# A planner of instruction order that makes five passes, ranks steps by latest begin and counts transfers at 320 GB/s

## The chip, the core and the metric

The kernel runs on one core of a Trainium2 chip. The metric is the device time in microseconds of one execution of the whole program; lower is better.

## The reference

Causal attention with a cumulated bias over 4 batches, 8 heads, 576 positions and head size 64; its output, as 2304 tokens of 512 values, goes through two layers with weights 512 x 2048 and 2048 x 512. Cut to what is computed:

```python
def _attn_ref(q, k, v, s):
    scores = scale * np.matmul(q, k.transpose(0, 1, 3, 2))
    cum = np.cumsum(np.maximum(s, 0.0), axis=-1)
    bias = -(cum[:, :, :, None] - cum[:, :, None, :])
    scores = np.where(causal, -1000000000.0, scores + np.minimum(bias, 0.0))
    scores = scores - np.max(scores, axis=-1, keepdims=True)
    attn = np.exp(scores)
    attn = attn / (np.sum(attn, axis=-1, keepdims=True) + 1e-09)
    return np.matmul(attn, v)

def _moe_ref(x, w_in, w_out):
    h = x @ w_in
    return (np.maximum(h, 0.0) + np.log1p(np.exp(-np.abs(h)))) @ w_out

def _moe2_ref(x, w_in, w_out, a, b):
    h = x @ w_in
    h2 = h * h
    P = a[0] + a[1] * h + a[2] * h2 + a[3] * h2 * h
    Q = 1.0 + np.abs(b[0]) * np.abs(h) + np.abs(b[1]) * h2
    return (P / (Q + 1e-06)) @ w_out
```

The weights come in as 64-bit floats.

## The kernel before

**Stages.** Attention is cut into parts (Part), one for a head and a range of its rows, in five segments: rows 0 to 255 of batch 0 in plain float32 (tiles gh, gl hold their probabilities), the rest of batch 0, and then the other batches. A part is scores on TensorE (L511, or L513 and L514), a mask with a row minimum on VectorE (L491, L497, L500), an exponential with row sums on ScalarE (L504), the reciprocal of the sum on VectorE (L505, L506), the normalisation on GpSimd (L507), transposes on TensorE (L574, L578, L589, L594) with copies out of PSUM (L559, L564, L565) and the product with v (L637). The first layer takes tokens in tiles of 256, 256 and four of 448, the second in six of 384; each tile has 16 units, one for 128 of the 2048 hidden columns. A unit is stage_a (L892 to L894, x by w_in, 12 matmuls), the activation (stage1: L990 to L994; stage2, stage3: L1030, L1032) and stage_b (L928 to L930 or L935 to L937, by w_out). All operands of the layers are split in a high and a low part that together stand for a float32, so that each product is three matmuls.

**Weights.** A half of a unit's weights (128 x 512) is loaded by load_w (L743) and put together from its 64-bit form in conv1: L758 on GpSimd, L759 on ScalarE, L760 and L765 on VectorE, the high part L769 on ScalarE, the low part w1l L770 on GpSimd. Low parts are stored (L779) and loaded again for later tiles (stream_l, L789); both stand on SyncE's queue. The first eight units of tile 0 need 16 halves; then come eight units of tile 1, and then both in turn.

**What sets the order.** Each engine works through its own line in order. The program is traced part by part and unit by unit, and each instruction has a priority, which is its place in the trace, moved by offsets with tc.high_priority: C1_OFF = 50 for conversions of the first layer's weights, PRIO, P_S2, P_PREP, P_CUM, P_SPLIT, P_A, P_ST1, P_ST3 for others. At the end of the trace plan() (L169) simulates all engines. Step (L97) gives each instruction a price by its kind and size; depend() (L139) gives what must come before what. plan() takes, again and again, the step that can begin first on any engine; among those of one engine that can begin at the same time, the lowest priority number goes first. Buffers of a tag are given in the order of the trace. The lines that come out are tied as they are, by after(), for all steps that the model begins before 530 us (L1226); later ones are ordered by the framework's scheduler from their priorities. The instructions up to keep_order() (L358), among them the loads of the first heads and of the cumulated sums, are tied by hand. Prices that the prediction uses:

```python
SHARED = 0.7
DMA_RATE, DMA_LATENCY = 260e3, 1.9
...
            self.done = 0.1 + 0.00064 * n if one else 0.147 + 0.00106 * n
...
            self.done = 0.17 + 0.00215 * n if wide else 0.28 + 0.00075 * n
...
            slow = SHARED * s.port * port[other] * max(0.0, min(clock[other] - t, busy))
...
            dma = max(dma, clock[s.engine]) + s.dma / DMA_RATE
            done = dma + DMA_LATENCY
```

n is the number of elements of a partition; the first pair of prices is VectorE's, the second GpSimd's.

Of the kernel before, what the change touches and what calls it, by code (L numbers as in the profile page):

```python
# [54 lines left out]
PSUM_TAGS = ("acc", "h", "at")  # L55
LATENCY = {("Activation", "Pool"): 0.08, ("DVE", "Pool"): 0.19, ("PE", "DVE"): 0.09}
ISSUE = {"SP": 0.5, "Activation": 0.12}
SHARED = 0.7
DMA_RATE, DMA_LATENCY = 260e3, 1.9


class Access:
# [34 lines left out]
class Step:  # L97


    def __init__(self, i, tied):  # L100
        self.i, self.tied = i, tied
        self.engine = str(i.engine).split(".")[-1]
        acc = [[Access(x) for x in xs if getattr(getattr(x, "bass_ap", None), "tensor", None) is not None]
               for xs in (i.outs, i.ins)]
        self.outs, self.ins = acc
        self.dma = self.port = 0
        n = self.outs[0].elements if self.outs else 1
        psum = any(x.psum for x in self.outs + self.ins)
        wide = len(self.ins) > 1 and self.ins[1].dims[1][1] > 1
        if "DMA" in i.opcode:  # L110
            self.dma = 4 * n * self.outs[0].dims[0][1]
            self.busy = ISSUE.get(self.engine, 0.5)
        elif self.engine == "PE":
            turn = n == 128 and self.ins[0].tile.startswith("ident")
            full = not turn and "32r" not in str(i.ins[0].bass_ap.dtype)
            self.busy = 0.109 if turn else 0.024 + 0.00162 * n if full else 0.012 + 0.000428 * n
            self.done = self.busy + 0.165
        elif self.engine == "Activation":
            self.done = 0.175 + 0.00086 * n + 0.095 * max(0, len(self.outs) + len(self.ins) - 2)
            self.busy = self.done - 0.1  # L120
        elif self.engine == "DVE" and n == 1:
            self.busy, self.done = 0.115, 0.155
        elif self.engine == "DVE":
            one = len(self.ins) < 2 and not psum and i.opcode != "TensorCopy"
            self.done = 0.1 + 0.00064 * n if one else 0.147 + 0.00106 * n
            self.busy = self.done - 0.08
            self.port = 0 if psum else 1
        elif self.engine == "Pool":
            self.done = 0.17 + 0.00215 * n if wide else 0.28 + 0.00075 * n
            self.busy = self.done - 0.03  # L130
            self.port = 1 if wide else 0.4
        else:
            self.busy = self.done = 0.1
# [5 lines left out]
def depend(steps):  # L139

    names = {s.i.name: k for k, s in enumerate(steps)}
    preds = [{} for _ in steps]
    seen, first = {}, {}
    for k, s in enumerate(steps):
        def add(j, result):
            if j != k:
                preds[k][j] = result or preds[k].get(j, False)

        for x in s.ins + s.outs:
            if not x.ordered:  # L150
                continue
            write = x in s.outs
            for j, w, y in seen.get(x.tile, ()):
                if (write or w or x.psum and steps[j].engine != s.engine) and x.meets(y):
                    add(j, True)
        for x in s.ins + s.outs:
            write = x in s.outs
            if write:
                seen[x.tile] = [a for a in seen.get(x.tile, ()) if a[0] == k or not x.covers(a[2])]
            seen.setdefault(x.tile, []).append((k, write, x))  # L160
            if x.pool:
                add(first.setdefault(x.tile, k), False)
        for n in s.tied:
            if n in names:
                add(names[n], False)
    return preds


def plan(instructions, tied, until):  # L169

    steps = [Step(i, tied.get(i.name, ())) for i in instructions if i.opcode != "TilePoolBoundary"]
    preds = depend(steps)
    n = len(steps)
    succ = [[] for _ in steps]
    open_ = [len(p) for p in preds]
    for k, p in enumerate(preds):
        for j, result in p.items():
            succ[j].append((k, result))
    tiles = [s.tiles() for s in steps]
    pool, users, queue = {}, {}, {}  # L180
    for k, s in enumerate(steps):
        for x in s.ins + s.outs:
            if x.pool and x.tile not in pool:
                pool[x.tile] = x.pool
                queue.setdefault(x.pool[0], []).append(x.tile)
        for t in tiles[k]:
            users[t] = users.get(t, 0) + 1
    slots = {tag: [0.0] * bufs for tag, bufs in pool.values()}
    head = {tag: 0 for tag in slots}
    last = {tag: 0.0 for tag in slots}  # L190
    held, freed = set(), {}
    ready, start = [0.0] * n, [0.0] * n
    engines = sorted({s.engine for s in steps})
    clock = {e: 0.0 for e in engines}
    wait = {e: [k for k, s in enumerate(steps) if s.engine == e and not open_[k]] for e in engines}
    lines = {e: [] for e in engines}
    dma = 0.0
    port = {e: 0 for e in engines}

    def earliest(k):  # L200
        t, need = ready[k], {}
        for x in tiles[k]:
            if x not in held:
                tag = pool[x][0]
                need[tag] = need.get(tag, 0) + 1
                ahead = queue[tag][head[tag]:head[tag] + need[tag]]
                if any(y not in held and y not in tiles[k] for y in ahead):
                    return None
                free = sorted(slots[tag])
                if len(free) < need[tag]:  # L210
                    return None
                t = max(t, free[need[tag] - 1], last[tag])
        return t

    for _ in range(n):
        best = None
        for e in engines:
            can = [(max(t, clock[e]), steps[k].i.bass_priority, k) for k in wait[e]
                   for t in (earliest(k),) if t is not None]
            if can and (best is None or min(can)[0] < best[0]):  # L220
                best = min(can)
        t, _, k = best
        s = steps[k]
        wait[s.engine].remove(k)
        for x in tiles[k]:
            if x not in held:
                tag = pool[x][0]
                slots[tag].sort()
                slots[tag].pop(0)
                held.add(x)  # L230
                last[tag] = max(last[tag], t)
                while head[tag] < len(queue[tag]) and queue[tag][head[tag]] in held:
                    head[tag] += 1
        busy, done = s.busy, getattr(s, "done", 0.0)
        if s.port:
            other = "Pool" if s.engine == "DVE" else "DVE"
            slow = SHARED * s.port * port[other] * max(0.0, min(clock[other] - t, busy))
            busy, done = busy + slow, done + slow
        port[s.engine] = s.port
        start[k], clock[s.engine] = t, t + busy  # L240
        if s.dma:
            dma = max(dma, clock[s.engine]) + s.dma / DMA_RATE
            done = dma + DMA_LATENCY
        else:
            done += t
        lines[s.engine].append(k)
        for j, result in succ[k]:
            if not result:
                at = t
            elif steps[j].engine == s.engine == "PE":  # L250
                at = clock["PE"]
            else:
                at = done + LATENCY.get((s.engine, steps[j].engine), 0.04)
            ready[j] = max(ready[j], at)
            open_[j] -= 1
            if not open_[j]:
                wait[steps[j].engine].append(j)
        for x in tiles[k]:
            users[x] -= 1
            freed[x] = max(freed.get(x, 0.0), done)  # L260
            if not users[x]:
                slots[pool[x][0]].append(freed[x] + 0.04)
    return [[steps[k].i for k in line if start[k] < until] for line in lines.values()]


@with_exitstack
def moe_chain_kernel(ctx, tc, qk0, qk, vv, s0, s, w1, w2, ab, out):
# [958 lines left out]
    for line in plan(nc.cur_bb.bb.instructions, tied, 530.0):  # L1226
        for prev, i in zip(line, line[1:]):
            after(i, prev)
# [55 lines left out]
```

## Time and profile before

| | |
|---|---|
| median of 3 runs | 1085.07 us (1083.73 to 1085.89) |
| the profiled execution | 1085.73 us, span 1083.9 us |
| TensorE, matmuls | 1033.3 us busy, 95% of the span |
| VectorE | 821.3 us, 76% |
| ScalarE | 826.3 us, 76% |
| GpSimd | 488.9 us, 45% |
| mean granted clock of TensorE | 0.982 of 2.4 GHz |

Busy times of engines overlap. A matmul's busy time includes what it takes longer at the lower clock. A wait of an engine is time in which it has nothing to run; the profile names the instruction that released it. Idle time of an engine that bounds nothing costs nothing. In the rows PE is TensorE, DVE VectorE, ACT ScalarE, POOL GpSimd, SP SyncE.

### The profile page before, as it was taken

The page shows a single profiled execution, that of the slowest core. Times are in us where ns is not written, and L with a number is a line of the kernel's source. Part 1 is how long each engine was busy: PE and PEld are TensorE (multiplying, and loading weights), DVE is VectorE, ACT ScalarE, POOL GpSimd, SP SyncE. Part 2 cuts the span into 40 slices and gives each one's busy share as a digit, 9 for nine tenths or more (in the row PEclk, how much of TensorE's full clock was granted, in tenths as well). Part 3 has the DMA queues.
Part 4 walks back from the last instruction along what each step waited for, and adds up shares of the span by engine and source line. Part 5 has one row for each costly group of instructions (what it writes and reads, how often), then busy time and mean ns, then how long its engine had stood idle before and what let it go on. Part 6 is the DMA issues. An engine that isn't in the chain of part 4 may idle for free.

```text
span 1083.9 us, 17808 instructions
## 1 busy us (share of the span) xinstructions
PE 1033.3 (95%) x5732; PEld 927.4 (86%) x5732; DVE 821.3 (76%) x1886; ACT 826.3 (76%) x1748; POOL 488.9 (45%) x541
## 2 busy tenths in 40 slices
PE   5787889999999999999999999999999999999998
PEld 3676789988888888888999988998999999999997
DVE  5898988778887798885677667777777676766765
ACT  4798888878888788776566546788787887887885
POOL 5786356551221122321344575544545454454543
PEclk9698889999999999999999999999999999999999
DMA  6856556576555473523787875301010010000000
GB/s 196 268 191 215 165 167 194 165 227 184 158 159 173 121 219 118 154 83 107 230 260 248 288 265 170 117 1 59 1 30 30 1 59 1 30 30 2 30 1 29
DMA packets 70333, 139.43 MB, mean 129 GB/s; under 512 B 8384, under 2 KB 24144, under 8 KB 70240
## 3 DMA queue, kind: packets, MB, share of 16 engines
q1 hardware_dynamic: 67696, 134.14, 38.8%
q10 hardware_dynamic: 2544, 4.16, 1.6%
q8 instruction: 45, 0.74, 0.3%
q14 instruction: 48, 0.39, 0.1%
HBM read 111.60 MB, written 22.61 MB: 124 GB/s over the span
## 4 chain that ended last, share of the span: by engine, by line
PE 77%; DVE 11%; ACT 4%; POOL 4%; issue 2%; DMA 2%; SPq 0%; POOLq 0%; ACTq 0%; DVEq 0%
PE h L893 7%; PE h L892 7%; PE h L894 7%; PE acc L937 6%; PE acc L935 6%; PE acc L936 6%; PE at L637 4%; PE acc L929 4%; PE acc L930 4%; PE acc L928 4%; PE at L892 3%; PE at L894 3%; PE at L893 3%; PE at L513 3%; PE at L514 2%
## 5 line engine op out<-in xcount | busy, mean ns | idle before, releaser
L892 PE MATMUL h<-xs,w1h 128*128 128x448 f32 (+1 forms) x352 | 121.1, 345 | 8.3 <-DVE e L994 7.4
L893 PE MATMUL h<-xs,w1h 128*128 128x448 f32 (+1 forms) x352 | 119.8, 340 | 0.4 <-DVE xs L862 0.4
L894 PE MATMUL h<-xs,w1l 128*128 128x448 f32 (+1 forms) x352 | 119.9, 341 | 0.2 <-POOL w1l L770 0.2
L928 PE MATMUL acc<-gh,w1h 128*128 128x448 f32 (+1 forms) x352 | 119.2, 339 | 0.1
L930 PE MATMUL acc<-gh,w1l 128*128 128x448 f32 (+1 forms) x352 | 118.7, 338 | 0.6 <-POOL w1l L770 0.6
L929 PE MATMUL acc<-gl,w1h 128*128 128x448 f32 (+1 forms) x352 | 119.0, 338 | 0.0
L935 PE MATMUL acc<-w2h,gh 128*128 128x512 f32 x288 | 113.3, 393 | 0.2 <-ACT gh L1030 0.2
L937 PE MATMUL acc<-w2h,gl 128*128 128x512 f32 x288 | 113.5, 394 | 0.0
L936 PE MATMUL acc<-w2l,gh 128*128 128x512 f32 x288 | 113.3, 393 | 0.0
L507 POOL TENSOR_SCALAR PA<-PA,stat 128x384 f32<-128x384 f32 (+3 forms) x112 | 68.9, 620 | 98.2 <-DVE stat L506 47.9
L1032 POOL TENSOR_TENSOR gl<-PA,gh 128x384 fp32r<-128x384 f32 x95 | 98.0, 1032 | 7.3 <-ACT gh L1030 5.0
L1003 POOL TENSOR_TENSOR tc<-tc,e 128x384 f32<-128x384 f32 x47 | 50.9, 1082 | 95.5 <-ACT tc L1001 95.5
L507 POOL TENSOR_SCALAR P<-P,stat 128x576 f32<-128x576 f32 x32 | 26.4, 825 | 137.2 <-DVE stat L505 69.1
L892 PEld LDWEIGHTS h<-xs,w1h 128*128 128x128 f32 x352 | 67.8, 193 | 14.1 <-DVE e L994 7.5
L565 DVE TENSOR_TENSOR ptl<-at,pth 128x320 fp32r<-128x320 f32 (+2 forms) x107 | 60.5, 568 | 18.1 <-ACT pth L564 16.8
L504 ACT ACTIVATE PA<-PA,stat 128x384 f32<-128x384 f32 (+3 forms) x112 | 63.8, 570 | 13.2 <-DVE stat L491 12.4
L893 PEld LDWEIGHTS h<-xs,w1h 128*128 128x128 f32 x352 | 67.8, 193 | 3.7 <-DVE xs L862 0.7
L894 PEld LDWEIGHTS h<-xs,w1l 128*128 128x128 f32 x352 | 67.5, 192 | 3.4 <-POOL w1l L770 0.4
L930 PEld LDWEIGHTS acc<-gh,w1l 128*128 128x128 f32 x352 | 66.2, 188 | 4.0 <-POOL w1l L770 1.2
L928 PEld LDWEIGHTS acc<-gh,w1h 128*128 128x128 f32 x352 | 66.5, 189 | 3.3 <-ACT w1h L769 0.3
L929 PEld LDWEIGHTS acc<-gl,w1h 128*128 128x128 f32 x352 | 66.4, 189 | 3.0
L1030 ACT ACTIVATE gh<-PA 128x384 fp32r<-128x384 f32 x96 | 50.4, 525 | 21.1 <-DVE PA L1018 17.8
(226 smaller groups left out, 3299.2 us busy)
## 6 DMA issues: line engine op xcount, KB each, us to landing
w1l<-l_d SPq DMA_DIRECT2D x148, 256.0 KB
raw<-in_w_dram SPq DMA_DIRECT2D x48, 512.0 KB
raw<-in_qk_dram SPq DMA_DIRECT2D x32, 384.0 KB
l_d<-w1l SPq DMA_DIRECT2D x32, 256.0 KB
raw64x<-in_w_dram SPq DMA_DIRECT2D x16, 512.0 KB
R<-in_vv_dram SPq DMA_DIRECT2D x16, 320.0 KB
raw<-in_qk_dram SPq DMA_DIRECT2D x8, 576.0 KB
out_dram<-yb SPq DMA_DIRECT2D x17, 256.0 KB
```

The source lines that it names most:

```text
L504: nc.scalar.activation(pt[:, 0:n], pt[:, 0:n], AF.Exp, bias=mn, scale=-1.0, accum_out=stat[:, i, 1:2])
L507: nc.gpsimd.tensor_scalar(pt[:, 0:n], pt[:, 0:n], stat[:, i, 2:3], 1.0, op0=ALU.mult, op1=ALU.mult)
L892: nc.tensor.matmul(h, wh[:, cs], xh, start=(k == 0), stop=False)
L893: nc.tensor.matmul(h, wh[:, cs], xl, start=False, stop=False)
L894: nc.tensor.matmul(h, wl[:, cs], xh, start=False, stop=(k == KD - 1))
L928: nc.tensor.matmul(o, wh[:, cs], gh, start=first and not both, stop=False)
L929: nc.tensor.matmul(o, wh[:, cs], gl, start=False, stop=False)
L930: nc.tensor.matmul(o, wl[:, cs], gh, start=False, stop=last and (not both or m % 2 == 1))
L935: nc.tensor.matmul(acc[m], gh[:, cs], wh, start=first, stop=False)
L936: nc.tensor.matmul(acc[m], gh[:, cs], wl, start=False, stop=False)
L937: nc.tensor.matmul(acc[m], gl[:, cs], wh, start=False, stop=last)
L1032: eng.tensor_tensor(gl, g, f(gh), op=ALU.subtract)
```

## The change

plan() is split into a class Planner with two functions. forward() is the simulation as before, with rank[k] in the place of the priority and HOLD = 0.0 as the time within which a later but lower-ranked step may be preferred. latest() goes back from the end of the last simulation and gives each step the latest begin at which what follows is not late: the next step on TensorE's line, the steps that need its result, and the first user of the buffer that it frees. plan() simulates five times: the first with the traced priorities, the others with the result of latest() after the pass before; the pass with the shortest modelled time gives the lines. Steps that begin before 530 us in it are tied, as before. Besides, the transfer rate in the model is 320 instead of 260 GB/s, and depend() keeps register moves, and affine selects, of an engine in their order. No instruction is added to the program or taken from it.

```diff
--- before.py
+++ after.py
@@ -55,8 +55,8 @@
 PSUM_TAGS = ("acc", "h", "at")
 LATENCY = {("Activation", "Pool"): 0.08, ("DVE", "Pool"): 0.19, ("PE", "DVE"): 0.09}
 ISSUE = {"SP": 0.5, "Activation": 0.12}
-SHARED = 0.7
-DMA_RATE, DMA_LATENCY = 260e3, 1.9
+SHARED, HOLD, ROUNDS = 0.7, 0.0, 5
+DMA_RATE, DMA_LATENCY = 320e3, 1.9
 
 
 class Access:
@@ -109,7 +109,7 @@
         wide = len(self.ins) > 1 and self.ins[1].dims[1][1] > 1
         if "DMA" in i.opcode:
             self.dma = 4 * n * self.outs[0].dims[0][1]
-            self.busy = ISSUE.get(self.engine, 0.5)
+            self.busy = self.done = ISSUE.get(self.engine, 0.5)
         elif self.engine == "PE":
             turn = n == 128 and self.ins[0].tile.startswith("ident")
             full = not turn and "32r" not in str(i.ins[0].bass_ap.dtype)
@@ -140,7 +140,7 @@
 
     names = {s.i.name: k for k, s in enumerate(steps)}
     preds = [{} for _ in steps]
-    seen, first = {}, {}
+    seen, first, moved = {}, {}, {}
     for k, s in enumerate(steps):
         def add(j, result):
             if j != k:
@@ -163,104 +163,160 @@
         for n in s.tied:
             if n in names:
                 add(names[n], False)
+        if s.i.opcode in ("RegisterMove", "TensorScalarAffineSelect"):
+            if s.engine in moved:
+                add(moved[s.engine], False)
+            moved[s.engine] = k
     return preds
 
 
+class Planner:
+    def __init__(self, instructions, tied):
...
+    def lag(self, k, j):
+        a, b = self.steps[k].engine, self.steps[j].engine
+        if a == b == "PE":
+            return 0.0
+        return self.after[k] + LATENCY.get((a, b), 0.04)
+    def forward(self, rank):
...
+        for _ in range(n):
+            best = None
+            for e in self.engines:
+                can = [(max(t, clock[e]), rank[k], k) for k in wait[e] for t in (earliest(k),) if t is not None]
+                if can:
+                    t0 = min(can)[0]
+                    pick = min((c for c in can if c[0] <= t0 + HOLD), key=lambda c: (c[1], c[0], c[2]))
+                    if best is None or pick[0] < best[0]:
+                        best = pick
...
+            busy, done = s.busy, s.done
+            if s.port:
+                other = "Pool" if s.engine == "DVE" else "DVE"
+                slow = SHARED * s.port * port[other] * max(0.0, min(clock[other] - t, busy))
+                busy, done = busy + slow, done + slow
+            port[s.engine] = s.port
+            self.start[k], clock[s.engine] = t, t + busy
+            self.end[k] = t + busy
+            if s.dma:
+                dma = max(dma, clock[s.engine]) + s.dma / DMA_RATE
+                self.after[k] = dma + DMA_LATENCY - self.end[k]
+            else:
+                self.after[k] = done - busy
...
+        return max(self.end)
+    def latest(self):
+        n = len(self.steps)
+        T = max(self.end)
+        late = [T - (self.end[k] - self.start[k]) for k in range(n)]
+        follow, reuse = {}, {}
+        for k, j in zip(self.lines["PE"], self.lines["PE"][1:]):
+            follow[k] = j
+        for x, y in self.slot_of.items():
+            if y is not None:
+                first = min(self.users[x], key=lambda k: self.start[k])
+                for k in self.users[y]:
+                    reuse.setdefault(k, []).append(first)
+        for k in sorted(range(n), key=lambda k: (-self.start[k], -k)):
+            busy = self.end[k] - self.start[k]
+            bound = late[k]
+            if k in follow:
+                bound = min(bound, late[follow[k]] - busy)
+            for j, result in self.succ[k]:
+                bound = min(bound, late[j] - busy - self.lag(k, j) if result else late[j])
+            for j in reuse.get(k, ()):
+                bound = min(bound, late[j] - busy - self.after[k] - 0.04)
+            late[k] = bound
+        return late
 def plan(instructions, tied, until):
...
-        for e in engines:
-            can = [(max(t, clock[e]), steps[k].i.bass_priority, k) for k in wait[e]
-                   for t in (earliest(k),) if t is not None]
-            if can and (best is None or min(can)[0] < best[0]):
-                best = min(can)
...
+    p = Planner(instructions, tied)
+    rank = [s.i.bass_priority for s in p.steps]
+    best = None
+    for _ in range(ROUNDS):
+        total = p.forward(rank)
+        if best is None or total < best[0]:
+            best = total, p.lines, p.start
+        rank = p.latest()
+    _, lines, start = best
```

## Rows read from the trace of the kernel before

**Rows 1.** Stretch: length, busy us of PE, PEld, DVE, ACT, POOL; PEclk, DMA share, GB/s.
```profile
...
0.00:27.00 27.00, 14.52 (x56) 10.70 (x56) 14.79 (x60) 13.24 (x38) 15.18 (x28) 1.00 0.64 195
27.00:120.00 93.00, 74.77 (x469) 65.34 (x469) 84.04 (x218) 76.93 (x177) 67.08 (x69) 0.87 0.66 217
120.00:217.00 97.00, 88.83 (x649) 84.42 (x650) 79.95 (x224) 83.72 (x221) 53.32 (x71) 0.93 0.55 174
217.00:530.00 313.00, 310.23 (x1849) 273.24 (x1848) 248.22 (x742) 244.65 (x554) 77.58 (x113) 1.00 0.53 157
530.00:1084.00 554.00, 544.94 (x2715) 493.66 (x2713) 394.31 (x645) 407.72 (x761) 275.73 (x263) 1.00 0.26 86
...
```

**Rows 2.** The same view, for 30 to 36 us.
```profile
...
30.00:36.00 6.00, 4.34 (x14) 3.38 (x12) 6.00 (x12) 4.32 (x12) 5.99 (x6) 0.50 0.91 281
...
```

**Rows 3.** TensorE's waits, 0 to 170 us: us in total, times, longest us.
```profile
...
PE acc L511 <- DMA raw<-cumc: 7.9, 1, 7.9
PE acc L574 <- POOL gh L507: 6.0, 3, 2.8
PE at L594 <- POOL P L507: 5.2, 3, 2.2
PE h L892 <- DVE e L994: 4.8, 4, 2.1
...
PE h L574 <- POOL gh L507: 1.3, 1, 1.3
...
PE at L574 <- POOL gh L507: 0.4, 1, 0.4
...
PE h L894 <- POOL w1l L770: 0.2, 1, 0.2
```

**Rows 4.** GpSimd's order of work: start us, us, instruction [idle before <- releaser].
```profile
...
24.70 1.26 POOL L770 TENSOR_TENSOR w1l<-tc,w1h 128x512 fp32r<-128x512 f32 x1
25.95 1.50 POOL L507 TENSOR_SCALAR gh<-gh,stat 128x256 f32<-128x256 f32 x1
...
30.40 3.53 POOL L770 TENSOR_TENSOR w1l<-tc,w1h 128x512 fp32r<-128x512 f32 x2
...
34.97 2.11 POOL L507 TENSOR_SCALAR gh<-gh,stat 128x128 f32<-128x128 f32 x2
...
46.40 1.32 POOL L770 TENSOR_TENSOR w1l<-tc,w1h 128x512 fp32r<-128x512 f32 x1 [3.14 <-ACT w1h L769]
...
```

**Rows 5.** TensorE's order of work, the same columns.
```profile
...
27.50 0.55 PE L574 MATMUL acc<-ident,gh 128*128 128x128 f32 x3 [2.09 <-POOL gh L507]
...
37.14 0.90 PE L574 MATMUL acc<-ident,gh 128*128 128x128 f32 x3 [2.79 <-POOL gh L507]
...
45.03 0.41 PE L892 MATMUL h<-xs,w1h 128*128 128x256 f32 x1
...
```

**Rows 6.** Groups by line, 44 to 120 us: count | busy us, mean ns | idle before.
```profile
...
L770 POOL TENSOR_TENSOR w1l<-tc,w1h 128x512 fp32r<-128x512 f32 x12 | 17.5, 1465 | 7.1 <-ACT w1h L769 7.1
L760 DVE SCALAR_TENSOR_TENSOR tc<-raw,tc 128x512 int32<-128x512 int32 x13 | 12.4, 958 | 0.7 <-ACT raw L759 0.6
L758 POOL TENSOR_SCALAR tc<-raw 128x512 f32<-128x512 f32 x14 | 11.9, 850 | 0.5
L765 DVE SCALAR_TENSOR_TENSOR tc<-raw,tc 128x512 int32<-128x512 int32 x13 | 11.5, 886 | 0.1
...
```

**Rows 7.** VectorE's order of work, the columns of rows 4.
```profile
...
30.97 1.84 DVE L483 TENSOR_TENSOR vs<-R,vs 128x640 fp32r<-128x640 f32 x1
32.73 1.75 DVE L760 SCALAR_TENSOR_TENSOR tc<-raw,tc 128x512 int32<-128x512 int32 x1
34.41 0.15 DVE L506 RECIPROCAL stat<-stat 128x1 f32<-128x1 f32 x1
...
```

**Rows 8.** The chain that ended last, in order of time: start us, us, what.
```profile
...
324.60 2.85 DMA w1l<-l_d
...
```

**Rows 9.** SyncE's queue, waits from 0 to 217 us, columns of rows 3.
```profile
...
SPq L779 <- POOL w1l L770: 59.7, 23, 10.5
...
```

More of the change, by code (lines that the diff above doesn't have):

```diff
@@ L165, in depend @@
                 add(names[n], False)
-    return preds
-def plan(instructions, tied, until):
[L171 to L216, printed above, removed]
-        for e in engines:
-            can = [(max(t, clock[e]), steps[k].i.bass_priority, k) for k in wait[e]
-                   for t in (earliest(k),) if t is not None]
-            if can and (best is None or min(can)[0] < best[0]):
-                best = min(can)
[L222 to L263, printed above, removed]
@@ L266, in moe_chain_kernel @@
+def plan(instructions, tied, until):
+    p = Planner(instructions, tied)
[7 more added lines that the diff above has]
+    _, lines, start = best
+    return [[p.steps[k].i for k in line if start[k] < until] for line in lines.values()]
 @with_exitstack
```

71 lines of the change are left out of this document (added).

## Prediction

> **What bounds the kernel now.** The views were read in this order: busy time by stretch, waits of the matmul engine, the order of work on GpSimd, VectorE and the matmul engine around its longest waits, then the prices of the steps that stood there. The stretches [rows 1] split the span in two. From 217 us on TensorE is busy for 310.2 of 313 us up to 530 and for 544.9 of 554 after that: 11.9 us idle in 867, with the clock at its upper level. Nothing that reorders other engines there can bring more than those few. Before 217 us it is busy for 14.5 of 27, 74.8 of 93 and 88.8 of 97 us: 38.9 us idle. In the last two stretches the granted clock is 0.87 and 0.93, a mix of both levels (1.2 and 2.4 GHz): (1 - 0.87) x 2 x 93 = 24 us and 0.07 x 2 x 97 = 13.6 us at the lower one. An example is the stretch in which the clock is 0.50 throughout after TensorE had waited much [rows 2]. A matmul then takes twice as long, so half of the TensorE work of those 38 us, at its busy shares of 0.80 and 0.92, is lost: 24 x 0.80 / 2 = 9.6 and 13.6 x 0.92 / 2 = 6.3, some 16 us. So all that better order could win before 217 us is 38.9 - 7.9 + 16 = 47 us; the 7.9 is the first wait of all, for the small load of the cumulated sums [rows 3], and stays (below).
>
> TensorE is not alone at its limit, though. VectorE is busy for 84.0 of the 93 us between 27 and 120, and 80.0 of 97 after that [rows 1]. If all its work of these stretches must stand before the same matmuls, the first can shrink by 9.0 us at most and the second, where ScalarE is busier, by 13.3. This is the real ceiling: 22 us and what the clock gives back.
>
> **What TensorE waits for.** Up to 170 us six rows, from 6.0 to 0.4 us, name the normalisation of the softmax on GpSimd (L507, tiles gh, PA and P) and sum to 14.5 us, 7.7 of them for gh; four waits for the softplus add on VectorE (L994) sum to 4.8 [rows 3]. These are short steps of attention and of stage 1 that stand in line behind conversion steps of the weights (L758, L760, L765, L770). The conversions were put ahead on purpose: conv1 is traced under C1_OFF = 50, so that in a tie it goes before attention steps traced up to 50 instructions earlier.
>
> **Part 1: the rank.** The change replaces the number that decides among steps which are ready at the same time. In the first pass it is still the traced priority with its hand-set offsets; in passes 2 to 5 it is the latest begin at which the step still doesn't delay the TensorE line of the pass before. The pass with the shortest modelled total is kept. HOLD is 0, so no engine waits for a more urgent step that isn't ready yet: only true backlogs are reordered, and a step that runs is not interrupted.
>
> Where a backlog stands can be read. Between 24.7 and 37.0 us GpSimd has no pause and alternates conversions with the normalisations [rows 4]; TensorE waits 2.09, 1.3 and 2.79 us for the latter [rows 3, 5], and its first matmul of the MLP is at 45.03 [rows 5]. The conversions ahead weren't urgent: the two L770 of 30.40 serve units that start after 45. Step by step: (a) the normalisation of 25.95 could take the place of the L770 before it (24.70): 1.25 us earlier. (b) The normalisation behind the wait of 1.3 us has one L758 ahead of it, 0.85 us by their mean [rows 6]. (c) The normalisation of 34.97 waits for a reciprocal at 34.41, which stands on VectorE behind L483 (1.84) and L760 (1.75) [rows 7], and then for its turn on GpSimd. Without the L760 the reciprocal is done 1.75 us sooner; GpSimd is by then inside an L770 that ends at 33.93, so that only some 1.0 to 2.0 us are won; I take 2.0, since the L770 goes back too. Sum 1.25 + 0.85 + 2.0 = 4.1 us. What is put back is hidden by GpSimd's pause of 3.14 us before 46.40 [rows 4]; without that cover it costs up to one L770 mean, 1.5 us [rows 6].
>
> From 54 to 170 us the same reading applies to 6.8 us of waits for L507 (14.5 less the 7.7 for gh) and the 4.8 for L994 [rows 3], but VectorE has only a tenth of its time free. I take a third of 11.6, 3.9 us; the bounds are 0 (all of it is capacity) and the 9.0 us that VectorE has free. Conversions that go back fall due within this stretch: for that I charge one L770 mean, 1.5 us, with bounds 0 and 16 conversions late (second rival).
>
> **Part 2: the clock.** Fewer waits mean fewer us at the lower level. I take 2.0 us of the 16, an eighth, as the waits removed (8.0) are a fifth of 38.9 and the stretch of 30 to 36 us stays thin anyway. The bounds are -4 (new waits lower it elsewhere) and +8 (half of it).
>
> **Part 3: transfers at 320 instead of 260 GB/s in the model.** A 256 KB reload costs 0.82 + 1.9 = 2.72 us in the new model and 2.91 in the old; the one on the chain took 2.85 [rows 8], between them. The stretch of 30 to 36 us moved 281 GB/s at a busy share of 0.91 [rows 2], 309 for full transfer engines (an estimate, 281 / 0.91). So the new rate is at least as true, and moves a planned arrival by 0.2 to 0.4 us. Steps are planned that much earlier. If a transfer is late by it, everything behind the waiting step on its engine (in-order) is late as well. SyncE's queue shows what such a wait holds: its stores of the low halves (L779) wait 59.7 us in 23 cases for L770, and loads of the next weights stand behind them [rows 9]. Where the new order brings L770 later, these loads come later. Conversions run ahead of their use, so I set this at 0, bounds -1 and +2.
>
> **Edits with one answer.** The tie between register moves and between affine selects only keeps their order. The instructions issued up to keep_order() are tied by hand, so the first wait of 7.9 us stays. Steps that the model begins after 530 us aren't fixed in either version, so the 9.1 us idle there [rows 1] stay, give or take 1. No instruction is added or taken away on the chip.
>
> **Sum.** 4.1 + 3.9 - 1.5 + 2.0 = 8.5 us. The profiled execution took 1085.73 us, of which 1083.9 are span. 1085.7 - 8.5 = 1077.2; that execution lies 0.7 above the median of the runs, so the forecast is **1076.5 us**, 0.8% less. With the good bounds of this forecast (4.1 + 6 + 4) it is 1071; with the poor ones (3 + 0 + 0) 1082.
>
> **Rivals.** First: **the order moves only who waits.** VectorE stays the bound from 27 to 120 us [rows 1], every conversion it postpones comes due within the same stretch, and the planner may even find the first pass the best, so that the change doesn't do what it says. Then the 4.1 us won before 45 us are handed back by 120: 1083 to 1087. For it speaks the 90% of VectorE; against it, that 44 to 120 us still has pauses on all four engines.
>
> Second, and on the other side: **conversions planned just in time come too late.** The ranks go by the model's prices. Those of one half of a weight tile are 0.69 for L760 and L765 each, 1.27 for L770 and 0.66 for L758 before any sharing; measured between 44 and 120 us are 0.958, 0.886, 1.465 and 0.850 [rows 6], 0.85 us more for a half. The L760 of 32.73 took 1.75 us [rows 7], 1.06 over its price, beside the second L770 of the row at 30.40, which ends at 33.93 [rows 4]; the model adds at most 0.7 of a step's own busy time, 0.43 us. The Trainium skill (SBUF — State Buffer, Who interferes with whom) says that the port pair shared by the two engines is an exclusive lock, and that a VectorE instruction with two SBUF inputs blocks wholly against a GpSimd one that reads SBUF, whichever issues second. The trace agrees in this row, where the L760 ends 0.55 us after the L770; by the rule each such collision would cost some 1.1 instead of 0.43 us. Priced by rows: the first eight units of tile 0 need 16 halves; 16 x 0.85 = 13.6 us, of which half is hidden at best, so +6.8 us and 1091.9, and with the clock falling again up to 1096. It decides from the point at which a conversion's lead over its matmul falls under 0.85 us. Against it: TensorE waited 0.2 us in all for low halves up to 170 us [rows 3], the conversions of 30.40 lead by more than 10 us, and with HOLD at 0 an idle GpSimd still takes them early.
>
> Third: **more than I count.** VectorE's free 9.0 and ScalarE's 13.3 us are mostly used and the clock stays up: 12 to 22 us, 1063 to 1073.
>
> **How the numbers follow.** Forecast (1071 to 1082) 0.46; first rival 0.15; second 0.24; third 0.15. The range should leave out 0.2: half of the second rival above (it spans 1086 to 1096, so 1090 leaves out some 0.12) and the better half of the third below (0.07). So 1066 to 1090. A measurement can tell some 0.2%, 2.2 us, from no change: faster is under 1082.9, slower over 1087.2. Faster: the forecast and the third, 0.61, and a little of the first's spread, 0.62; same: most of the first, 0.14; slower: the second, 0.24.
>
> **What would show it.** Right: the first MLP matmul (L892) at some 40 to 42 us instead of 45.03; waits for L507 under 9 us in all; in GpSimd's order around 25 to 37 us normalisations ahead of L770; a clock above 0.87 between 27 and 120; the stretches after 217 only shifted. Wrong: TensorE waits for w1l or w1h (L769, L770), 0.2 us for L770 now, grow to several us; VectorE's busy time from 27 to 120 grows by collisions; or the time is lost or won after 217 us, where I see no room.

## The result and the profile after

The changed kernel took 1071.65 us in the median of 4 runs (1070.87 to 1072.39), the kernel before 1084.4 us beside it (1081.02 to 1085.89): a ratio of 0.9887, with a 95% interval of 0.9861 to 0.9912. In a later set of runs it was 1073.54 against 1083.66 us, 0.9913 (0.9892 to 0.9933). The forecast was 1076.5, the range 1066 to 1090. One execution of one experiment below took 1660.81 us at a mean granted clock of 0.56, far below all others; it counts in no time and no ratio. The profiled execution after took 1071.19 us, with a span of 1069.4; the one before was 1085.73, so the two profiles differ by 14.5 us, where the medians differ by 12.8 and 10.1.

In the file after, lines of the kernel stand 56 further down: L507 became L563, L758 L814, L760 L816, L765 L821, L770 L826, L892 L948, L994 L1050. The stretches that answer to [rows 1], with the columns told there:

```profile
0.00:27.00 27.00, 15.24 (x60) 11.48 (x61) 16.99 (x66) 14.56 (x40) 13.50 (x28) 1.00 0.63 201
27.00:120.00 93.00, 77.21 (x496) 67.70 (x497) 83.63 (x226) 78.86 (x183) 71.27 (x69) 0.91 0.64 211
120.00:217.00 97.00, 88.84 (x705) 85.61 (x704) 85.94 (x231) 89.55 (x239) 71.19 (x79) 1.00 0.64 207
217.00:530.00 313.00, 311.61 (x1836) 277.76 (x1835) 244.98 (x736) 241.40 (x542) 72.66 (x110) 1.00 0.53 161
530.00:1070.00 540.00, 530.31 (x2644) 480.28 (x2642) 381.28 (x631) 401.05 (x747) 270.38 (x257) 1.00 0.24 81
```

TensorE's idle time before 217 us is 11.8 + 15.8 + 8.2 = 35.7 us where it was 38.9: little less. The granted clock, 0.87 and 0.93 before, is 0.91 and 1.00. Between 120 and 217 us TensorE was busy for the same 88.8 us and did 705 matmuls instead of 649. GpSimd was busy there for 71.2 instead of 53.3 us, VectorE for 85.9 instead of 80.0.

TensorE's waits up to 170 us, against [rows 3] (us in total, times, longest):

```profile
PE acc L567 <- DMA raw<-cumc: 8.1, 1, 8.1
PE at L650 <- POOL P L563: 4.6, 4, 1.9
PE h L948 <- DVE e L1050: 3.4, 2, 1.7
...
PE acc L645 <- POOL PA L563: 1.7, 3, 0.8
PE acc L630 <- POOL gh L563: 1.6, 3, 0.6
PE at L634 <- POOL PA L563: 1.4, 1, 1.4
PE acc L650 <- POOL P L563: 1.3, 1, 1.3
PE h L948 <- ACT w1h L825: 1.1, 1, 1.1
...
PE acc L986 <- POOL w1l L826: 0.9, 1, 0.9
...
PE acc L634 <- POOL PA L563: 0.6, 1, 0.6
...
PE h L630 <- POOL gh L563: 0.2, 1, 0.2
```

The waits for gh fell from 7.7 to 1.6 + 0.2 = 1.8 us. Those for P and PA rose from 6.8 (5.2 in [rows 3], and the two lines below) to 4.6 + 1.7 + 1.4 + 1.3 + 0.6 = 9.6. The other two waits before:

```profile
PE acc L589 <- POOL PA L507: 0.9, 1, 0.9
...
PE acc L594 <- POOL P L507: 0.7, 1, 0.7
```

In all the waits for this line are 11.4 us, where I had said that under 9 would show the forecast right. GpSimd's order (start us, us, instruction, what it waited for) shows the first of these changes, against [rows 4]:

```profile
24.20 1.74 POOL L814 TENSOR_SCALAR tc<-raw 128x512 f32<-128x512 f32 x2
27.54 2.83 POOL L563 TENSOR_SCALAR gh<-gh,stat 128x256 f32<-128x256 f32 x4 [1.59 <-DVE stat L562]
30.33 1.27 POOL L826 TENSOR_TENSOR w1l<-tc,w1h 128x512 fp32r<-128x512 f32 x1
31.70 0.71 POOL L814 TENSOR_SCALAR tc<-raw 128x512 f32<-128x512 f32 x1
32.38 1.33 POOL L563 TENSOR_SCALAR gh<-gh,stat 128x256 f32<-128x256 f32 x2
```

The four normalisations from 27.54 on run before the first w1l is made, which is at 30.33 instead of 24.70, and GpSimd has a pause of 1.59 us for VectorE instead of a line of conversions. The last normalisation of gh ends at 33.7 us, where it was 40.4. The first matmul of the MLP comes at 38.87 us, where it was 45.03 [rows 5]:

```profile
38.87 0.37 PE L948 MATMUL h<-xs,w1h 128*128 128x256 f32 x1
```

**Where the time went, by units.** Windows of time compare different work, so the two traces were cut at the first matmul of the same units of the first layer: unit 0, 4, 8, 12 and 32, counted by the four matmuls of L892 (L948) that each unit has; unit 32 is the first of a tile of 448. Columns as in [rows 1]. Before:

```profile
0.00:45.03 45.03, 26.57 (x92) 19.64 (x93) 30.49 (x99) 25.27 (x65) 30.26 (x42) 0.82 0.68 211
45.03:61.25 16.22, 13.80 (x101) 12.67 (x100) 13.77 (x36) 14.31 (x35) 12.42 (x12) 0.98 0.67 241
61.25:98.70 37.45, 31.49 (x215) 27.83 (x214) 34.52 (x90) 31.71 (x75) 26.70 (x27) 0.95 0.69 232
98.70:150.87 52.17, 43.26 (x266) 39.01 (x264) 44.57 (x137) 43.19 (x109) 24.02 (x32) 0.84 0.49 156
150.87:230.32 79.45, 74.63 (x597) 72.31 (x597) 67.53 (x164) 70.04 (x184) 52.06 (x63) 1.00 0.60 188
```

After:

```profile
0.00:38.87 38.87, 25.73 (x97) 19.62 (x97) 26.84 (x98) 24.68 (x64) 22.05 (x38) 0.87 0.70 230
38.87:62.37 23.50, 18.66 (x128) 16.92 (x127) 20.33 (x54) 20.18 (x50) 16.91 (x16) 0.93 0.59 184
62.37:96.63 34.26, 28.25 (x201) 24.64 (x200) 33.60 (x82) 30.71 (x71) 30.98 (x29) 1.00 0.69 228
96.63:140.65 44.02, 35.81 (x250) 32.06 (x249) 39.81 (x125) 37.67 (x97) 29.22 (x31) 0.96 0.62 202
140.65:218.41 77.76, 73.89 (x598) 72.41 (x597) 67.39 (x167) 70.76 (x188) 57.27 (x63) 1.00 0.61 196
```

Of a stretch, length less PE's busy time is idle time, and busy time by (1 - clock) is what the lower level cost: a share of 2 x (1 - clock) of the time at half speed loses half the work of that share. (It takes TensorE as equally busy at both levels.) Worked out so:

| until the first matmul of | before: us, idle, cost of clock | after: us, idle, cost of clock | lead of after |
|---|---|---|---|
| unit 0 | 45.03, 18.5, 4.8 | 38.87, 13.1, 3.3 | 6.2 |
| unit 4 | 61.25, 2.4, 0.3 | 62.37, 4.8, 1.3 | -1.1 |
| unit 8 | 98.70, 6.0, 1.6 | 96.63, 6.0, 0.0 | 2.1 |
| unit 12 | 150.87, 8.9, 6.9 | 140.65, 8.2, 1.4 | 10.2 |
| unit 32 | 230.32, 4.8, 0.0 | 218.41, 3.9, 0.0 | 11.9 |
| sum (before rounding) | 40.6 idle, 13.6 clock | 36.1 idle, 6.1 clock | |

The lead at unit 32 is 11.9 us, and the sums differ by 4.5 of idle time and 7.5 of clock. The busy time itself says the same without the working: up to unit 32 TensorE was busy for 189.75 us with 1271 matmuls before, and for 182.34 us with 1274 after, 7.4 us less. The largest step, 8.1 us between units 8 and 12, holds 0.7 of idle time and 5.5 of clock; the rest is that fewer matmuls stand there (250 against 266).

### The profile page after: what moved, and what is told of

It reads as the page before. It is cut to its first block, busy times and chain, and to the rows that moved or that the text cites. A ratio compares the mean times of both kernels' runs of the same rounds, so it can differ in the third digit from the quotient of the medians.

```text
span 1069.4 us, 17821 instructions
## 1 busy us (share of the span) xinstructions
PE 1023.2 (96%) x5732; PEld 922.8 (86%) x5732; DVE 812.8 (76%) x1886; ACT 825.4 (77%) x1748; POOL 499.0 (47%) x541
## 4 chain that ended last, share of the span: by engine, by line
PE 70%; DVE 11%; ACT 7%; DMA 4%; POOL 3%; issue 3%; SPq 1%; POOLq 0%; DVEq 0%; ACTq 0%
PE h L948 6%; PE h L949 6%; PE h L950 6%; PE acc L993 5%; PE acc L991 5%; PE acc L992 5%; PE at L693 4%; PE acc L986 4%; PE acc L985 4%; PE acc L984 4%; PE at L948 3%; PE at L950 3%; PE at L949 3%; PE at L569 3%; PE at L570 2%
## 5 line engine op out<-in xcount | busy, mean ns | idle before, releaser
L948 PE MATMUL h<-xs,w1h 128*128 128x448 f32 (+1 forms) x352 | 119.8, 342 | 6.8 <-DVE e L1050 5.7
L563 POOL TENSOR_SCALAR PA<-PA,stat 128x384 f32<-128x384 f32 (+3 forms) x112 | 74.8, 673 | 88.4 <-DVE stat L562 26.3
L563 POOL TENSOR_SCALAR P<-P,stat 128x576 f32<-128x576 f32 x32 | 25.7, 804 | 134.5 <-DVE stat L561 44.6
L948 PEld LDWEIGHTS h<-xs,w1h 128*128 128x128 f32 x352 | 66.5, 189 | 11.8 <-DVE e L1050 7.5
L949 PEld LDWEIGHTS h<-xs,w1h 128*128 128x128 f32 x352 | 66.8, 190 | 4.1 <-DVE xs L918 1.3
L1072 DVE SCALAR_TENSOR_TENSOR tc<-tc,e 128x384 f32<-128x384 f32 x48 | 27.5, 573 | 51.0 <-ACT e L1071 49.8
```

The lines of the kernel that those rows point to most:

```text
L563: nc.gpsimd.tensor_scalar(pt[:, 0:n], pt[:, 0:n], stat[:, i, 2:3], 1.0, op0=ALU.mult, op1=ALU.mult)
L948: nc.tensor.matmul(h, wh[:, cs], xh, start=(k == 0), stop=False)
L949: nc.tensor.matmul(h, wh[:, cs], xl, start=False, stop=False)
```

## Experiments

There are twelve runs, ten of edited kernels and one more of each of the two kernels. Each is compared with the kernel before on the same chip; the ratio's interval is 95%.

**The two halves of the change.** One simulation, new rate:

```diff
-SHARED, HOLD, ROUNDS = 0.7, 0.0, 5
+SHARED, HOLD, ROUNDS = 0.7, 0.0, 1
```

> One simulation instead of five, so the traced priorities rank the steps as before; only the transfer rate of 320 GB/s in the model (and the tie of register moves) is left of the change. Theory (the ranks make the gain): within 2.2 us of the kernel before, with the first MLP matmul near 45 us and a granted clock near 0.84 between units 8 and 12. Rival (the rate makes it): 1070 to 1076 us.

1077.63 us, 0.9952 (0.993 to 0.9974). Neither: the rate alone made 0.48%, against my theory that it does nothing. It doesn't do it by an earlier start. Unit 0 comes at 48.58, later than in the kernel before (rows from unit 0 to 8, to 12 and to 32 below the first):

```profile
0.00:48.58 48.58, 26.38 (x96) 19.93 (x97) 36.58 (x108) 29.09 (x72) 34.42 (x46) 0.79 0.74 236
48.58:103.94 55.36, 46.57 (x334) 42.68 (x333) 53.31 (x135) 48.80 (x116) 38.72 (x39) 0.97 0.58 202
103.94:146.19 42.25, 34.77 (x243) 31.16 (x242) 39.56 (x119) 36.56 (x95) 21.25 (x29) 0.96 0.59 180
146.19:224.79 78.60, 74.29 (x597) 72.36 (x597) 63.50 (x163) 69.38 (x181) 55.07 (x63) 1.00 0.61 192
```

Idle time is 42.8 us up to unit 32, 2.2 more than before; the clock costs 8.3 instead of 13.6. So the new rate only led the same rule to another order, one that lost less clock in this profile. The register moves that the change keeps in order have no part in it: with and without that tie the planner writes the same lines in one simulation, at 260 and at 320 GB/s.

Five simulations, old rate:

```diff
-DMA_RATE, DMA_LATENCY = 320e3, 1.9
+DMA_RATE, DMA_LATENCY = 260e3, 1.9
```

> Five simulations with latest begins, but transfers at 260 GB/s in the model as before. Theory (the ranks make the gain): 1070 to 1077 us, first MLP matmul at 38 to 41 us. Rival (the rate makes it): 1082 to 1087 us.

1078.72 us, 0.9965 (0.9944 to 0.9986), above the theory's range and below the rival's, with unit 0 at 37.06. Idle time falls to 37.5 us, the cost of the clock to 7.7 (worked out as above). The two halves are worth 4.9 and 3.8 us alone and 10 to 13 together. An early unit 0 is not what the time follows: the rate alone has the latest, this run the earliest, and the rate alone gains no less.

**Where in the order the gain arises.** The new order for an early stretch only, then the traced priorities:

```diff
...
+    prio = rank
+    p.forward(prio)
+    p.forward(p.latest())
+    rank = [t - 1e6 if t < 81.0 else r for t, r in zip(p.start, prio)]
+    total = p.forward(rank)
...
```

> The new order for the steps that the model begins before 81 us (unit 8 of the first layer), the traced priorities after that. The model, which knows no clock, sees the whole gain of the change here. Theory A (about 3 us are idle time won before unit 8, the other 9 are clock that the new order wins between units 8 and 12 by itself): 1079 to 1083 us, with a granted clock near 0.84 between units 8 and 12. Rival B (what is won later follows from the state that the early order leaves): 1070 to 1075 us, clock above 0.93 there.

1073.97 us in the median of six executions, 0.9914 (0.9883 to 0.9945): in the range of the rival B. The clock between units 8 and 12 has no reading here. The mean clock of the six whole executions is 0.986 to 1.000, 0.994 in the middle, as in the changed kernel (0.990 to 0.997).

The other way round, the old rule up to unit 8 and the new ranks after it:

```diff
...
+    p.forward(rank)
+    rank = [t - 1e6 if t < 86.0 else r for t, r in zip(p.start, p.latest())]
+    total = p.forward(rank)
...
```

> The order of the first simulation up to unit 8 (steps that the model begins before 86 us), the latest begins after that. Theory A (the order between units 8 and 12 wins the clock): 1073 to 1078 us, granted clock above 0.93 between units 8 and 12. Rival B (the early order makes it): 1081 to 1087 us, clock near 0.84 there.

1077.54 us, 0.9947 (0.9924 to 0.997). This lies in theory A's range, but the ranges were set against the kernel before, at 260 GB/s. The run to compare with is the new rate alone (1077.63 us), whose lines are the same up to about unit 8, and it is no better than that. The clock between units 8 and 12 is 0.92, where the rate alone had 0.96 (stretches up to unit 0 and from unit 8 to 12):

```profile
0.00:49.89 49.89, 30.17 (x97) 23.16 (x98) 36.48 (x110) 30.07 (x73) 34.89 (x47) 0.73 0.72 232
104.98:147.96 42.98, 35.48 (x244) 31.89 (x243) 38.20 (x119) 36.43 (x95) 23.58 (x29) 0.92 0.54 176
```

Theory A falls: the new ranks gain nothing after unit 8, though much of the clock that the change wins shows only there. With the run before this one, what is won follows from the early order. The first row shows something else. Up to unit 0 the order is that of the rate alone, but here 19.7 us are idle and 8.1 are lost to the clock, there 22.2 and 5.5. So one order can lose more or less clock in another execution, and here its idle time changed by as much the other way.

**The favour of the conversions.** The kernel before with one number changed:

```diff
-C1_OFF = 50
+C1_OFF = 0
```

> The kernel before with C1_OFF = 0 instead of 50: one simulation, 260 GB/s, but conversions of the weights no longer go ahead of attention steps traced up to 50 instructions earlier. Theory of the prediction's part 1 (this favour is what the ranks put right): first MLP matmul (L892) at 38 to 41 us and 1075 to 1080 us. Rival (the favour is needed further on, and only due times tell when): first matmul earlier too, but 1081 to 1088 us.

1077.91 us, 0.9953 (0.9932 to 0.9974), with the first matmul of the MLP at 38.42:

```profile
38.42 0.56 PE L892 MATMUL h<-xs,w1h 128*128 128x256 f32 x1
```

This is what part 1 of the prediction said: the hand-set favour held up the first attention heads. Dropping it takes the waits for gh from 7.7 to 4.8 us up to 170 us, and gives the early start of the change and some half of its gain (0.47% of 0.87 to 1.13%). Not run: no favour and 320 GB/s in one simulation, whose modelled total is 1033.4 us against the change's 1031.7. How much of the gain needs the ranks is therefore open.

**Is it this plan or any plan of the kind?** The planner's own total of a simulation is at hand for each kernel, so plans of nearly equal total were run: the fourth and the third simulation of the change in the place of the second (`if _ == 3` and `if _ == 2` where the best is kept), and five simulations at 300 GB/s.

> The changed kernel with the fourth simulation taken instead of the second: its modelled total is 1031.80 against 1031.65 us. Theory A (the chip's time follows the modelled total): 1070 to 1074 us. Theory B (plans of equal modelled total scatter on the chip by several us, as the model knows no clock): away from 1071.7 by 3 us or more, with the difference in the clock between units 0 and 12.

1073.59 us, 0.992 (0.9905 to 0.9936).

> The third simulation taken, modelled total 1032.53 us. Theory A: 1071 to 1075 us. Theory B: anywhere from 1069 to 1080, and not in the order of the modelled totals with the other passes.

1071.22 us, 0.9899 (0.9884 to 0.9914).

> The changed kernel with transfers at 300 instead of 320 GB/s in the model; the kept pass has a modelled total of 1029.74 us, 1.9 less than the change's. Theory A: 1068 to 1072 us. Theory B: anywhere from 1069 to 1080. If 320 GB/s itself is what counts, between the 1078.7 of 260 and the 1071.7 of 320, some 1074.

1069.03 us, 0.9881 (0.9862 to 0.99). All three times lie in theory A's ranges. Only the fourth simulation tells the theories apart: it is 1.9 us from the change's first median of 1071.7, where B asked for 3 or more. The other two times fit B as well, and the third simulation has the higher total but the lower time of the two, though their intervals touch. The rate of 320 is not special: 300 is at least as good. Up to unit 32 the 300 GB/s plan has 35.1 us idle and loses 3.9 to the clock:

```profile
0.00:38.63 38.63, 24.82 (x97) 18.78 (x97) 26.98 (x93) 23.27 (x61) 21.84 (x38) 0.91 0.66 217
38.63:102.38 63.75, 54.35 (x368) 47.02 (x367) 60.99 (x156) 57.46 (x135) 50.23 (x47) 0.97 0.65 216
102.38:139.11 36.73, 29.88 (x208) 25.25 (x206) 35.52 (x108) 31.00 (x82) 21.87 (x26) 1.00 0.57 183
139.11:218.23 79.12, 74.10 (x600) 72.60 (x598) 67.37 (x168) 71.12 (x188) 59.82 (x66) 1.00 0.62 206
```

**Plans that the model likes still better, and repeats.** Ranks of the fifth simulation up to 60 us and the traced priorities after that, at 320 GB/s; the same with the third simulation at 300:

```diff
+    p.forward([t - 1e6 if t < 60.0 else r for t, r in zip(p.start, prio)])
```

> Ranks of the fifth simulation for the steps that it begins before 60 us, the traced priorities after that, 320 GB/s: modelled total 1028.37 us, 3.3 less than the change's. If the chip's time follows the modelled total as in the runs so far (1.6 us for each modelled us under the 1037.8 of the kernel before): 1066 to 1070 us. Rival (the traced priorities after the first stretch bring the clock down again, as the 1074.8 of the other run of this kind suggests): 1072 to 1077 us.

1072.46 us, 0.9901 (0.9868 to 0.9934).

> The same kind with the ranks of the third simulation, at 300 GB/s: modelled total 1028.52 us. By the modelled total 1066 to 1070 us; by the rival 1072 to 1077 us.

1074.48 us, 0.9919 (0.9895 to 0.9944). Both lie in the rival's range: 3 modelled us less than the change brought nothing. The rival's reason doesn't hold for the second: its clock is 1.00 from unit 4 to unit 32, with 33.2 us idle there and before, and it leads the change's second profile by 3.3 us at unit 32. It gives that back between units 32 and 48, which take it 126.1 us and the change's second profile 122.1: eight matmuls more stand there (739 against 731), which the change had done before unit 32, and 0.9 us more are idle. So most of its lead was work put off.

The two kernels unchanged:

> The kernel before, unchanged, for a second profile. Theory (idle time belongs to the order, the clock in part to chance): TensorE's idle time up to unit 32 within 1.5 us of the first profile's 40.6, while what the lower clock costs there may differ from its 13.6 us by several us; time 1080 to 1087 us. Rival (both belong to the order): 13.6 within 1.5 us as well.

> The changed kernel, unchanged, for a second profile and its time beside the next two on one chip. Theory: idle time up to unit 32 within 1.5 us of 36.0; cost of the lower clock 4 to 9 us, below the kernel before in any execution; 1070 to 1073 us.

1083.21 us for the kernel before in one execution, 1073.54 in the median of four for the changed one, just above its range (0.9913, against the 1083.66 us of seven executions of the kernel before). The second profile of before, between units 8 and 12, is nearly the first one again, clock and all; the second one of after (units 8 to 12, then 16 to 32) differs from the first by one further fall of the clock, 0.03 x 60.3 = 1.8 us:

```profile
98.80:150.99 52.19, 43.18 (x266) 38.96 (x264) 44.82 (x137) 43.27 (x109) 24.12 (x32) 0.84 0.49 156
```

```profile
96.75:140.76 44.01, 35.84 (x249) 32.06 (x248) 39.82 (x125) 37.65 (x97) 29.21 (x31) 0.96 0.62 200
157.05:220.08 63.03, 60.34 (x474) 59.12 (x473) 49.23 (x129) 55.88 (x147) 46.14 (x50) 0.97 0.58 187
```

Up to unit 32, over the stretches of the table, the kernel before has 39.9 us idle and loses 13.4 to the clock (40.6 and 13.6 in the first profile); the changed one 35.8 and 7.6 (36.1 and 6.1). In these two pairs the rival is right. But two profiles are few, and the mean clock of whole executions says how far it holds: it is 0.978 to 0.989 in 38 executions of the kernel before, and 0.990 to 0.997 in 8 of the changed one. The two do not overlap, so the clock does belong to the order, while single executions of one order differ by up to 0.011. In the executions of the new ranks after unit 8, a mean clock of 0.983 went with 1078.7 us (the mean of three) and 0.987 with 1076.2 (of three), some 6 us for 0.01 (an estimate). By that the 0.008 to 0.010 between the middles of the two orders are 5 to 6 us, about half of the gain, and the first pair of profiles shows the clock's part rather too large.

In the second pair the lead at unit 32 is 229.6 - 220.1 = 9.5 us, and nothing changes after it (9.3 at the first matmul of unit 120). The 2.6 us by which the first pair differs after 218 us does not come back, and is not shown to belong to the order.

**All plans together.** The planner's modelled total and the measured ratio:

| kernel | modelled total, us | ratio to before |
|---|---|---|
| before | 1037.8 | 1 |
| five simulations, 260 | 1035.9 | 0.9965 |
| new ranks after unit 8 | 1035.2 | 0.9947 |
| rate alone | 1035.1 | 0.9952 |
| no favour (C1_OFF = 0) | 1033.8 | 0.9953 |
| third simulation | 1032.5 | 0.9899 |
| fourth simulation | 1031.8 | 0.9920 |
| the change (twice) | 1031.7 | 0.9887, 0.9913 |
| new order until unit 8 | 1030.8 | 0.9914 |
| five simulations, 300 | 1029.7 | 0.9881 |
| early ranks, 300 | 1028.5 | 0.9919 |
| early ranks, 320 | 1028.4 | 0.9901 |

From 1037.8 to 1032 the chip follows the model, and gains between 1.3 and 2.2 us for each modelled one (the change itself 10 to 13 us for 6.1). Below 1032 it doesn't follow any more: 0.988 to 0.992 in any order. The 300 GB/s plan has the lowest time, but its interval overlaps that of the change.

## Why the prediction was right, point by point

**The bound and the sign** were right: at unit 32, some 220 us in, the lead was 11.9 of the 14.5 us of the first pair of profiles, and all of the second pair's. The waits for gh fell by 5.9 us, where I had 4.1 for the first stretch, and the start of the MLP moved by 6.2 us, to 38.87 (forecast: 40 to 42). Removing the favour alone (C1_OFF = 0) shows the cause of the early start.

**The second term was wrong.** For 54 to 170 us I took a third of 11.6 us of waits as gain, 3.9. The waits for P, PA and L994 were 6.8 + 4.8 before and are 9.6 + 3.4 now: 1.4 us more. The conversions that left the first 45 us are made from 45 to 120, and some steps beside them get longer. Groups from 44 to 120 us, each shape by itself, before and after (count, busy us, mean ns, idle before):

```profile
L1032 POOL TENSOR_TENSOR gl<-e,gh 128x256 fp32r<-128x256 f32 x8 | 6.6, 820 | 4.1 <-ACT gh L1030 4.1
...
L507 POOL TENSOR_SCALAR PA<-PA,stat 128x512 f32<-128x512 f32 x7 | 6.0, 858 | 4.9 <-DVE stat L506 4.0 <-PE at L513 0.9
...
L507 POOL TENSOR_SCALAR PA<-PA,stat 128x384 f32<-128x384 f32 x7 | 5.3, 761 | 4.5 <-DVE stat L506 2.8 <-DVE stat L505 0.9 <-ACT raw L759 0.8
```

```profile
L826 POOL TENSOR_TENSOR w1l<-tc,w1h 128x512 fp32r<-128x512 f32 x15 | 22.9, 1528 | 7.1 <-ACT w1h L825 6.9
...
L1088 POOL TENSOR_TENSOR gl<-e,gh 128x256 fp32r<-128x256 f32 x8 | 7.7, 957 | 0.2 <-ACT gh L1086 0.2
L563 POOL TENSOR_SCALAR PA<-PA,stat 128x512 f32<-128x512 f32 x6 | 7.6, 1275 | 1.9 <-PE acc L570 0.9 <-ACT w1h L825 0.6 <-DVE stat L562 0.4
...
L563 POOL TENSOR_SCALAR PA<-PA,stat 128x384 f32<-128x384 f32 x7 | 5.8, 825 | 1.9 <-DVE stat L562 1.9
```

Fifteen w1l instead of the twelve of [rows 6]. The normalisation of PA takes 1275 instead of 858 ns at 512 columns and 825 instead of 761 at 384, the low part of the activation 957 instead of 820; that of P is unchanged (955 and 952), and L760 got shorter (792 and 958). That it is the shared ports that lengthen some of them is argued from the prediction's row of a collision, not tried, and that these steps made the longer waits is not shown either. The lead of 6.2 us is gone by unit 4. That is what the first rival said, but only in part: of the 7.3 us lost there 2.4 are idle time, 1.0 is clock, and 3.9 are matmuls done there instead of later (128 against 101, most of the difference attention's). My charge of 1.5 us for the give-back was too small. Idle time in all fell by 4.5 us in the first pair of profiles and 4.1 in the second, where my three terms 4.1 + 3.9 - 1.5 had 6.5.

**The clock was the term most wrong in size.** I took 2.0 of some 16 us (13.6 in the finer stretches above); it gave 7.5 us in the first pair and 5.8 in the second (13.4 against 7.6), inside its bounds of -4 and +8. I made the clock a share of the waits removed. In the traces it isn't: between units 8 and 12 idle time is 8.9 and 8.2 us, the cost of the clock 6.9 and 1.4. The profile of the rate alone has more idle time than before and 5.3 us less of clock, though its first stretch came out otherwise in the other kernel with the same early lines. What decides that a fall comes is not shown. In stretches of 6 us, before: 114 to 126 us; after: 78 to 90 us:

```profile
114.00:120.00 6.00, 4.34 (x30) 3.40 (x28) 5.86 (x16) 4.66 (x11) 3.28 (x4) 1.00 0.58 197
120.00:126.00 6.00, 5.18 (x22) 4.27 (x23) 4.81 (x16) 4.17 (x11) 1.56 (x3) 0.57 0.81 286
```

```profile
78.00:84.00 6.00, 3.53 (x23) 2.63 (x22) 5.94 (x11) 5.53 (x14) 5.36 (x5) 1.00 0.68 200
84.00:90.00 6.00, 5.88 (x45) 5.41 (x45) 5.87 (x14) 4.88 (x11) 5.51 (x6) 1.00 0.63 230
```

In the first case the clock is at its lower level for most of the stretch that follows 4.34 us of work; in the second it stays up after 3.53. The Trainium skill (TensorE: Matmul & The Clock Gate, What's actually happening) counts the ramp to the upper level as under 1% of a typical kernel span, speaking of the warm-up of a kernel. Here the clock falls again and again, and all of it together costs 13.6 of 1083.9 us, 1.3%, before, and 6.1 of 1069.4, 0.6%, after; in these two profiles the difference is over half of the lead at unit 32.

**Part 3** was wrong in its size: 0 with bounds -1 and +2, measured -4.9 by itself. Its reasoning looked at when transfers land. What counted is that another rate in the model makes another order: its lines differ within TensorE's first dozen steps. That any such number would do is not shown; 260, 300 and 320 were tried.

**The rivals.** The first (the order moves only who waits) holds up to unit 8 and falls after. The second didn't come: waits for w1h and w1l grew from 0.2 to 1.1 + 0.9 = 2.0 us up to 170 us, far from 6.8, and none of the plans was slower than before. VectorE's busy time from 27 to 120 us is 83.6 against 84.0, so that no growth of collisions shows on VectorE; on GpSimd some steps got longer. The third came near the size by the wrong road: VectorE's free time was not used up between 27 and 120; it was used between 120 and 217, and the clock did about half or more.

**The sum.** Forecast 8.5 us, measured 12.8 and 10.1 in the medians. The idle terms were too large (6.5 together, against 4.5 and 4.1), and the clock's was too small (2.0, against 7.5 and 5.8). That the sum came out near is in part luck; what it had right are the bound, the sign and the first term.

## What to carry to other kernels

A list scheduler that ranks by latest begin corrects hand-set favours whose cost has moved elsewhere; the quickest check of such a favour is to set it to zero, which gave 5 us here. (Whether no favour and the new rate would do without the ranks was not run.) A model's total is a good guide over a difference of some 0.5% and none below that: among plans within 4 modelled us of each other, the chip has to choose. When two orders are compared, cut both traces at the same units of work and part the difference into idle time and cost of the clock, since the second can be the larger one and follows from the order too. It also differs between executions of one order, so that it takes more than one profile.

## What was unexpected of the hardware

The same order met the same falls of the clock in another execution: 0.84 between units 8 and 12 in both profiles of the kernel before, 0.96 in both of the changed one. This is no rule: up to unit 0 two kernels with the same early lines had 0.79 and 0.73. And similar idle time cost very different clock: 33 to 43 us of idle time up to unit 32 went with 3.9 to 13.6 us lost, not in the same order (42.8 and 8.3 for the rate alone, 40.6 and 13.6 for the kernel before).
